# One core, an FFT convolution beside a state-space scan: the hand-planned order of steps is replaced by a finer one, with six pooled buffer slots and a swap issued from two queues

## The chip, the cores and the metric

The kernel runs on one core of a Trainium2 chip. The metric is device time in microseconds (us); a time given for the kernel is the median of several executions. The profile is of one execution and gives the span from its first to its last instruction.

The engines are PE (TensorE, matrix products into PSUM), DVE (VectorE), ACT (ScalarE), POOL (GpSimd) and SP (SyncE). In this kernel POOL and SP do nothing but issue DMA transfers, apart from a few constants that POOL makes at the start.

## The reference, cut to what matters

There are two independent halves on sequences of 2048 steps with 1024 channels; the outputs are laid side by side.

```
# A: a 4-tap shift filter, a gate, and a long causal convolution by FFT
k_shift = sum_t k_pad[:, t:t+S, :] * shift_k[:, ks-1-t]
kv = k_shift * v
y  = irfft(rfft(pad(kv)) * rfft(pad(ssm_k)))[:S] + kv * ssm_D
a  = q * y
# B: a complex diagonal state-space layer, 1024 states
Bu = x @ B_bar.T ;  h = Lam_bar * h + Bu[t] ;  hseq = stack(h)
b  = 2 * Re(hseq @ C.T) + x * Dskip
return concatenate([a, b], axis=-1)
```

## The kernel before, in words

The whole program is a list of small steps written out by hand in the string `ORDER` (lines 65 to 164 of the kernel before). Each word names a step, its indices and the buffer slots that it takes: `U.3.1:p6` is step `U` for chunk 3, part 1, in PSUM slot p6; `lh.5:h0` is a load into slot h0. The loop at L728 reads the words from left to right and calls the step, so the string fixes the order of the instructions on each engine. Between engines there is no common order: an engine runs ahead until the next instruction in its own list has to wait for data or for a slot whose former tenant is still being read. So a load that stands late in the string may be issued long before its neighbours, if SP has nothing to wait for.

Half B goes in 16 chunks of 128 time steps. For chunk i:

- `x.i` (L441) loads the chunk transposed, by a DMA transpose on SP.
- `U.i.jp` (L453), four steps of 32 matmuls, 128x128 each, multiplies by B (`BT`); `ue.i.jp` (L455) is the ACT copy out of PSUM.
- `r1` and `r2` (L465, L474) rotate into real form on DVE, `sc` (L483) is the scan, two instructions, one for the real and one for the imaginary half, with the carry into the next chunk (L487, L488, added in `r2` at L476), and `r3`, `r4` (L465, L495) rotate back.
- `y.i.dh.part` (L506, L511) multiplies by C (`CT`) and adds the skip term; `ye` (L521) copies out on ACT and `yst` (L523) stores, issued by POOL.

Half A goes in stages that each need all of the stage before:

- `kp` and `vp` (L529, L537) load rows of k and v. `kvm` (L546) multiplies by the four filter taps, and `kva` (L553, L555, L556) sums the taps and multiplies by v: three DVE instructions in one step. `am` (L565) is the first short transform on PE, `ae` (L574) the ACT copy, and `ast` (L576) stores to the DRAM scratch `Ys_kv`, issued by POOL.
- `hl`, `hT`, `hc`, `hm`, `he`, `hst` (L580 to L624) do the same for the filter `ssm_k`, into `Ys_h`.
- Second stage, 32 groups g. `lh`, `lk` (L634) load two groups of `Ys_h`, `Ys_kv` in one transfer of 512 KB, and `lw` (L629) the weights of two groups, all issued by SP. `sh`, `sk` (L641) transform; `she`, `ske` (L651, L660) copy out on ACT. `sw.g` (L665, L666) is the swap: the tile `hab` holds a spectrum of 128 partitions (real part in 64, imaginary part in 64), and two transfers from SBUF to SBUF write a copy with the halves exchanged. Both are issued by POOL. `pr.g` (L671) multiplies the two spectra on DVE, and `sa.g` (L680) transforms back; `sae` (L689) copies out and `vst` (L693) stores to the scratch `Vs`.
- Third stage: `vl` (L698) loads from `Vs`, `a3` (L710) finishes the transform, `a3e` (L718) copies out, `qm` (L722) multiplies by q (`qp`, L703), `ost` (L726) stores.

At the start there are `ld_par`, `ld_w`, `wb`, `wbe` (parameters and filter taps), `bl`, `bT`, `bc` (load, transpose and copy of B into `BT`), `cl`, `cT`, `cc`, `cx` (the same for C, `cx` by DMA transpose) and `tabA1`, `sin1`, `eo`, `stt`, `z1`, `z2` (rotation tables).

Slots: p0 to p7 are the PSUM banks, b0 to b14 SBUF tiles of 256 KB, a0 to a10 of 512 KB, m0 and m1 the products of DVE, w0 to w2 the weights. A pool `a1` holds `kring` (rows of k) and the taps `wbc`; when its last reader is done, pool `a2` takes its place with the slots h0 to h2 and k0 to k2, which serve `lh` and `lk` alone (L633).

Of the kernel before, what the change touches and what calls it, by code (L numbers as in the profile page):

```python
# [14 lines left out]
ALU = mybir.AluOpType  # L15
# [7 lines left out]
NG = 32  # L23
# [51 lines left out]
ae.1.0:b8 cx.5.0 cT.3.0:p0 ast.0.1 ae.1.2:b13 U.2.3:p1 kvm.2:m1 cc.3.0 hl.2.0:a4 ae.1.3 cT.0.0:p7 ae.1.1 ast.1.1 cT.3.1:p2 lw.0:w0 ue.2.3 r2.0:a5
hT.0.1:p6 ast.1.0 cc.0.0 cT.2.0:p0 kva.2:b14 hT.0.2:p3 cc.3.1 hT.0.3:p5 cc.2.0 U.3.0:p1a0 hl.1.1:a6 hc.0.1:b11 sc.0 hc.0.3:b10 am.2.0:p7 am.2.1:p2
am.2.2:p0 am.2.3:p6 ae.2.0:b12 cx.6.1 hm.0.3.0:p5 ae.2.1 hm.0.3.1:p7 ae.2.2:b7 hm.0.3.2:p2 ast.2.0 ae.2.3 x.4:b6 cT.0.1:p0 he.0.3.2:b5 U.3.1:p6
ast.2.1 cc.0.1 he.0.3.0:b14 kvm.3:m0 kp.3 he.0.3.1 U.3.2:p2 ue.3.1 hst.0.3.0 ue.3.0 hc.0.2:b13 r3.0:m1 U.3.3:p0 x.6:b4 ue.3.2 ue.1.3 hm.0.2.0:p5
ue.3.3 hm.0.2.1:p7 hd.0 hm.0.1.0:p6 r4.0 hm.0.3.3:p1 he.0.2.0:b8 hm.0.0.0:p3 x.5:b12 hm.0.0.1:p2 he.0.1.0:b10 hm.0.2.2:p4 hm.0.2.3:p0 he.0.0.0:b7
hm.0.1.1:p5 r1.1:m1 y.0.0.0:p6 he.0.0.1 he.0.1.1 y.0.0.1 hst.0.0.0 he.0.3.3 he.0.2.1 x.7:b13 y.0.0.2 he.0.2.2:b14 r2.1:a7 hst.0.3.1 he.0.2.3 y.0.0.3  # L80
hl.2.1:a9 lw.2:w1 hm.0.0.2:p3 sc.1 hm.0.0.3:p2 hst.0.2.1 hT.1.0:p5 ye.0.0:b0 hT.1.1:p1 lw.1:w2 hm.0.1.2:p7 y.0.1.0:p4 hst.0.2.0 y.0.1.1 hst.0.1.0
he.0.0.2:b7 y.0.1.2 x.9:b3 he.0.0.3 y.0.1.3 r1.2:m1 hm.0.1.3:p0 ye.0.1 hT.1.2:p6 hst.0.0.1 hc.1.0:b11 hT.1.3:p3 U.4.0:p2a10 vp.7:a5 hc.1.3:b5 hd.1
r2.2:a3 yst.0 hc.1.2:b14 hm.1.0.0:p4 hm.1.0.1:p5 sc.2 ue.4.0 vp.3:a6 hm.1.0.2:p3 hm.1.0.3:p6 U.4.1:p2 he.0.1.2:b11 he.0.1.3 he.1.0.0:b8 hst.0.1.1
he.1.0.1 U.4.2:p7 ue.4.1 hst.1.0.0 hc.1.1:b10 U.4.3:p0 ue.4.2 r3.1:m1 he.1.0.2:b7 hm.1.1.0:p4 hm.1.1.1:p5 ue.4.3 hm.1.1.2:p2 hm.1.1.3:p1 he.1.0.3
hm.1.3.0:p7 r4.1 hm.1.3.1:p3 hm.1.3.2:p0 he.1.1.2:b10 hT.2.0:p6 hst.1.0.1 he.1.1.3 hm.1.3.3:p2 kva.3:b0 he.1.1.0:b5 y.1.0.0:p1 he.1.1.1 hst.1.1.1
y.1.0.1 y.1.0.2 he.1.3.2:b11 r3.2:m1 hst.1.1.0 vp.6:a8 he.1.3.3 y.1.0.3 y.1.1.0:p4 hst.1.3.1 ye.1.0:b8 r1.3:m0 y.1.1.1 am.3.0:p5 hc.2.0:b2 am.3.1:p0
# [12 lines left out]
hst.3.2.0 ue.6.1 kva.8:b2 hc.3.0:b5 hm.3.1.0:p6 hm.3.1.1:p7 hm.3.1.2:p4 ast.7.1 ue.6.2 hm.3.1.3:p2 hT.3.3:p5 he.3.1.0:b8 U.6.3:p3 he.3.1.1 r4.4
hc.3.3:b11 hst.3.1.0 kvm.9:m0 he.3.1.2:b10 y.4.0.0:p0 he.3.1.3 ue.6.3 am.8.0:p1 hst.3.1.1 am.8.1:p6 ae.8.0:b14 am.8.2:p7 am.8.3:p5 kvm.10:m1 y.4.0.1  # L100
ae.8.1 ae.8.2:b1 ast.8.0 y.4.0.2 ae.8.3 y.4.0.3 ast.8.1 kva.9:b2 kp.7 y.4.1.0:p4 ye.4.0:b8 y.4.1.1 kva.10:b10 am.9.0:p2 x.11:b14 am.9.1:p3 ae.9.0:b6
am.9.2:p1 am.9.3:p6 y.4.1.2 ae.9.1 ae.9.2:b2 y.4.1.3 ast.9.0 ae.9.3 kvm.11:m0 hm.3.3.0:p7 ast.9.1 ye.4.1 am.10.0:p5 am.10.1:p0 am.10.2:p2 ae.10.0:b1
hm.3.3.1:p3 yst.4 hm.3.3.2:p1 ae.10.1 am.10.3:p6 hm.3.3.3:p4 ae.10.2:b10 U.9.0:p5a10 kvm.12:m1 ast.10.0 ae.10.3 he.3.3.2:b11 ast.10.1 he.3.3.3
U.9.1:p0 he.3.3.0:b6 hd.3 hst.3.3.1 ue.9.0 kva.11:b2 he.3.3.1 hm.3.0.0:p2 hst.3.3.0 ue.9.1 hm.3.0.1:p6 hm.3.0.2:p1 hm.3.0.3:p4 he.3.0.0:b8 U.7.0:p7a6
he.3.0.1 kva.12:b1 he.3.0.2:b5 hst.3.0.0 he.3.0.3 am.11.0:p5 ue.7.0 am.11.1:p3 am.11.2:p0 am.11.3:p2 ae.11.0:b10 hst.3.0.1 U.7.1:p6 kvm.13:m0 ae.11.1
ae.11.2:b11 ae.11.3 ast.11.0 U.7.2:p1 ue.7.1 ast.11.1 kvm.14:m1 U.7.3:p4 ue.7.2 kva.13:b2 am.12.0:p7 ue.7.3 am.12.1:p5 am.12.2:p3 am.12.3:p0
ae.12.0:b6 U.8.0:p2a0 ae.12.1 kva.14:b8 ae.12.2:b5 ast.12.0 ae.12.3 am.13.0:p6 ue.8.0 am.13.1:p1 ast.12.1 am.13.2:p4 am.13.3:p7 ae.13.0:b10 U.9.2:p5
r1.5:m0 ae.13.1 ae.13.2:b11 ast.13.0 ae.13.3 am.14.0:p3 ue.9.2 am.14.1:p0 ast.13.1 am.14.2:p2 am.14.3:p6 ae.14.0:b1 kvm.15:m1 U.8.1:p1 ae.14.2:b2
ae.14.1 ae.14.3 ast.14.0 U.8.2:p4 ue.8.1 r2.5:a3 ast.14.1 lh.0:h0 lh.1:h1 lh.2:h2 kva.15:b6 U.8.3:p7 ue.8.2 U.9.3:p5 ue.8.3 sc.5 am.15.0:p3 ue.9.3
am.15.1:p2 am.15.2:p0 sh.0.0:p6 ae.15.0:b8 sh.0.1:p1 sh.1.0:p4 ae.15.1 am.15.3:p7 sh.1.1:p5 ae.15.2:b5 U.11.0:p3a4 lh.4:h0 ast.15.0 ae.15.3 she.0.0:a9  # L110
ast.15.1 she.0.1 r1.6:m0 sh.2.0:p2 she.1.0:a2 sh.2.1:p0 sw.0 sh.4.0:p7 she.1.1 sh.4.1:p6 sh.5.0:p1 she.4.0:a8 sh.5.1:p4 sh.3.0:p5 she.5.0:a7 lh.3:h2
# [55 lines left out]
def full_kernel(ctx, tc, A_q, A_k, A_v, A_shift_k, A_ssm_k, A_ssm_D, B_x, B_Lre, B_Lim, B_Bre, B_Bim,  # L167
                B_Cre, B_Cim, B_log_dt, B_Dskip, out, cfg=None):
    c = dict(CFG)
# [83 lines left out]
    def k4(name, shape):  # L253
        return rtile(ring, "a", name, shape)
# [115 lines left out]
    def z2():  # L370
        nc.scalar.mul(Z2[:, 2, :, :], Z2[:, 0, :, :], -1.0)
        for n_ in ("vc", "vs", "rn", "ang"):
            st.pop(n_)
# [419 lines left out]
```

## Time and profile before

| what | value |
|---|---|
| time, three executions | 390.65, 391.42, 395.95 us; median 391.42 us |
| span of the profiled execution | 394.4 us (its own time is not marked among the three) |
| PE busy, matmuls | 366.3 us, 93% of the span, 3529 matmuls |
| DVE busy | 331.7 us, 84% |
| ACT busy | 280.4 us, 71% |
| POOL busy | 126.9 us, 32% |
| bytes moved by DMA | 101.38 MB, mean 257 GB/s |
| transfers issued by SP: share of the 16 DMA engines' span | 54.5%, 58.73 MB |
| transfers issued by POOL: the same | 33.1%, 42.10 MB |

Matmuls overlap each other, so a busy PE is not the same as a PE that starts a matmul as often as it can. The spacing from one start to the next, in a stretch without waits, says what a matmul costs. The chain of waits gives this spacing, since it merges matmuls that follow each other. "PEld" is the load of a matmul's weights, which overlaps the matmuls. In "windows" rows the columns are: stretch, its length, busy time (and count) of each engine, granted TensorE clock, busy share of the DMA engines, GB/s.

### The profile page before, as it was taken

What the parts mean: (1) busy time and instruction counts of PE and PEld (TensorE: products, weight loads), DVE (VectorE), ACT (ScalarE), POOL (GpSimd) and SP (SyncE); (2) the same over time, 40 slices, a digit from 0 to 9 for tenths busy, and PEclk for the clock granted to TensorE, in tenths of its full rate; (3) what the DMA queues carried; (4) which work ended last, traced back from release to release, by engine and by line L of the source; (5) the groups of instructions that cost most, each with busy time, mean ns of one, the idle gap of its engine ahead of it and who ended that gap; (6) DMA issues with size and microseconds to landing.
All of it is one profiled execution on the core that took longest, in us unless ns stands there. A gap on an engine that the chain in (4) does not pass through costs nothing.

```text
span 394.4 us, 8923 instructions
## 1 busy us (share of the span) xinstructions
PE 366.3 (93%) x3529; PEld 246.4 (62%) x3529; DVE 331.7 (84%) x335; ACT 280.4 (71%) x519; POOL 126.9 (32%) x220
## 2 busy tenths in 40 slices
PE   4998998999988999999899699899998989999994
PEld 2898886775737858897366244455546458685441
DVE  4766999899989999999999979889956971999941
ACT  4899997676649969769289559589693994344642
POOL 3000124574716765425213233233240341020142
PEclk9999999999999999999999989999998999999999
DMA  6999999999986767368999997999989868458895
GB/s 192 313 250 290 328 234 280 297 239 373 303 199 225 220 190 249 125 199 295 270 269 296 276 239 244 236 330 268 321 244 284 253 161 295 161 181 285 292 359 216
DMA packets 59076, 101.38 MB, mean 257 GB/s; under 512 B 31102, under 2 KB 33150, under 8 KB 59036
## 3 DMA queue, kind: packets, MB, share of 16 engines
q1 hardware_dynamic: 45308, 58.73, 54.5%
q0 software_dynamic: 13728, 42.10, 33.1%
q8 instruction: 27, 0.44, 0.5%
q14 instruction: 13, 0.11, 0.1%
HBM read 52.57 MB, written 33.55 MB: 218 GB/s over the span
## 4 chain that ended last, share of the span: by engine, by line
PE 23%; issue 19%; DMA 12%; POOL 5%; ACT 3%; DVE 3%; POOLq 0%; SPq 0%; ACTq 0%; DVEq 0%
PE ps_y L506 7%; PE ps_a L641 5%; PE ps_a L680 5%; PE ps_u L453 5%; DMA l2k<-Ys_kv 4%; DMA l2h<-Ys_h 3%; DMA wts<-a_c_W 2%; POOL out_dram L726 2%; DMA hab<-hab 2%; ACT hab L651 1%; POOL Ys_kv L576 1%; DMA Ys_kv<-ysb 1%; DVE mt L546 1%; ACT x L660 1%; PE ps_a L565 0%
## 5 line engine op out<-in xcount | busy, mean ns | idle before, releaser
L506 PE MATMUL ps_y<-CT,h 128*128 128x512 bf16 x512 | 127.2, 381 | 1.3 <-DVE h L495 1.3
L453 PEld LDWEIGHTS <-BT 128*128 128x128 bf16 x2048 | 118.6, 99 | 6.1 <-issue 1.8
L453 PE MATMUL ps_u<-xT,BT 128*128 128x128 bf16 x2048 | 122.0, 220 | 0.4
L506 PEld LDWEIGHTS <-h 128*128 128x128 bf16 x512 | 46.0, 98 | 49.9 <-DVE h L495 2.2
L483 DVE TENSOR_TENSOR_SCAN h<-rtab,h 128x1024 bf16<-128x1024 f32 x32 | 71.5, 2274 | 0.2
L455 ACT CAST u<-ps_u 128x512 bf16<-128x512 f32 x64 | 39.9, 645 | 23.1 <-PE ps_u L453 21.5
L624 POOL DMA_DIRECT2D Ys_h<-ysbh x64 | 46.1, 723 | 23.4 <-ACT ysbh L617 20.6
L671 DVE TENSOR_TENSOR hab<-x,hab 128x2048 bf16<-128x2048 bf16 x32 | 38.8, 1222 | 17.4 <-DMA hab<-hab 11.0
L576 POOL DMA_DIRECT2D Ys_kv<-ysb x32 | 17.5, 549 | 87.2 <-ACT ysb L574 87.0
L465 DVE TENSOR_TENSOR mt<-u,Z 128x4096 bf16<-128x4096 bf16 x16 | 36.6, 2286 | 10.5 <-ACT u L455 10.2
L689 ACT CAST vsb<-ps_a 128x512 bf16<-128x512 f32 x64 | 36.0, 638 | 7.8 <-PE ps_a L680 7.8
L660 ACT CAST x<-ps_a 128x512 bf16<-128x512 f32 x64 | 36.9, 665 | 5.9 <-PE ps_a L641 5.8
L651 ACT CAST hab<-ps_a 128x512 bf16<-128x512 f32 x64 | 35.9, 679 | 7.1 <-PE ps_a L641 7.1
L617 ACT CAST ysbh<-ps_a 128x512 bf16<-128x512 f32 x64 | 34.6, 633 | 8.9 <-DMA Ys_h<-ysbh 5.2
L574 ACT CAST ysb<-ps_a 128x512 bf16<-128x512 f32 x64 | 34.3, 634 | 8.8 <-DMA Ys_kv<-ysb 6.1
L521 ACT CAST yo<-ps_y 128x512 bf16<-128x512 f32 x32 | 19.2, 611 | 26.9 <-PE ps_y L506 25.2
L465 DVE TENSOR_TENSOR mt<-h,Z 128x4096 bf16<-128x4096 bf16 x16 | 36.5, 2284 | 0.0
L680 PE MATMUL ps_a<-hab,wts 128*128 128x512 bf16 x128 | 32.4, 379 | 3.8 <-DVE hab L671 3.5
L546 DVE TENSOR_TENSOR mt<-kring,wbc 128x4096 bf16<-128x4096 bf16 (+3 forms) x16 | 29.9, 1884 | 3.4 <-DMA kring<-in_A_k_dram 3.4
L665 POOL DMA_DIRECT2D hab<-hab x32 | 16.8, 526 | 47.1 <-ACT hab L651 45.0
L511 PE MATMUL ps_y<-Dd,xT 128*128 128x128 bf16 x128 | 28.0, 219 | 0.0
L641 PEld LDWEIGHTS <-wts 128*128 128x128 bf16 x128 | 12.1, 99 | 21.0 <-DMA wts<-a_c_W 3.9
(110 smaller groups left out, 448.0 us busy)
## 6 DMA issues: line engine op xcount, KB each, us to landing
Ys_kv<-ysb POOLq DMA_DIRECT2D x32, 256.0 KB, 3.8
Ys_h<-ysbh POOLq DMA_DIRECT2D x64, 128.0 KB, 4.3
l2h<-Ys_h SPq DMA_DIRECT2D x16, 512.0 KB, 6.7
hab<-hab POOLq DMA_DIRECT2D x64, 128.0 KB, 6.7
l2k<-Ys_kv SPq DMA_DIRECT2D x16, 512.0 KB, 6.6
Vs<-vsb POOLq DMA_DIRECT2D x16, 512.0 KB, 4.9
vv<-Vs SPq DMA_DIRECT2D x32, 256.0 KB, 4.2
hk<-in_A_ssm_k_dram SPq DMA_DIRECT2D x8, 512.0 KB, 8.7
```

Source lines behind the costliest of these rows:

```text
L453: nc.tensor.matmul(pu[:, w, jl, :], BT[:, 2 * jp + jl, w, d, :], xT[:, d, :], start=(d == 0), stop=(d == ND - 1))
L455: E["ue"] = lambda i, jp: nc.scalar.copy(st["u", i][:, :, 2 * jp:2 * jp + 2, :], st.pop(("pu", i, jp))[:])
L465: nc.vector.tensor_mul(m, s_, win(Z))
L483: nc.vector.tensor_tensor_scan(gf[:, a * W:(a + 1) * W], rt1, gf[:, a * W:(a + 1) * W], 0.0, ALU.mult, ALU.add)
L506: nc.tensor.matmul(py[:], h[:, 1 - w, j, :], CT[:, j, w, dh * 512:(dh + 1) * 512], start=(j == 0 and w == 0), stop=(j == NJ - 1 and w == 1))
L617: nc.scalar.copy(st["yh", qd, n4, w // 2][:, :, w % 2, :], st.pop(("pa", qd, n4, w))[:].rearrange("p (c d) -> p c d", c=2))
L624: gpd(Ys_h[cc, n0:n0 + 2, :, qd * DQ:(qd + 1) * DQ].rearrange("n k d -> k n d"), t_[:, cc, :, :])
L651: nc.scalar.copy(st["hab", g][:, 0, cols], pt[:])
L660: nc.scalar.copy(st["x16", g][:, w * 512:(w + 1) * 512], st.pop(("ps", "l2k", g, w))[:])
L671: nc.vector.tensor_mul(hab[:], st.pop(("x16", g))[:].unsqueeze(1).to_broadcast([P, 2, D]), hab[:])
L680: nc.tensor.matmul(pt[:], st["w", gq][:, gi, 1 + a, :], hab[:, a, w * 512:(w + 1) * 512], start=(a == 0), stop=(a == 1))
L689: nc.scalar.copy(st["vsb", gq][:, gi, w * 512:(w + 1) * 512], st.pop(("ps", "v", g, w))[:])
```

## The change

- The string `ORDER` is written anew: 1722 words for 1565 before. Every transfer, matmul, copy and vector instruction of before is still there, as often as before.
- Steps are cut finer. `U` takes one state block of 16 matmuls for 32 (same PSUM tile, same single copy `ue`). `kva` becomes `kva`, `kvb`, `kvc`. The scan becomes `sc.i.0`, `sc.i.1`, then `cm`, `ca` (the carry), and `rc` is the addition of the carry. Other steps may now stand between these.
- The slots h0 to h2 and k0 to k2 go, and a11 to a16 come in pool `a2`. `lh` and `lk` take any slot a0 to a16, and so may `u`, `hab`, `vsb`, `vv`, `qt` and the others of that size.
- The swap's first half is issued by SP, in the same queue as the loads; the second half stays with POOL.
- `st.pop` becomes `st[...]` and the unused option `actsw` goes; neither makes an instruction.

```
-CFG = {'kr': 8, 'bdve': 4, 'actsw': ()}
+CFG = {'kr': 8, 'bdve': 4}
+NA = 11
...
-ld_par ld_w:a0a1 ld_G bl.2.0:b0 ld_sd bl.0.1:b1 bl.2.1:b2 ld_F x.0:b3 wb.4:p0 bl.3.0:b4 wb.0:p1 bl.7.1:b5 wbe.4 par_T:p2 bl.5.0:b6 wbe.0 bl.5.1:b7
+ld_w:a0a1 wb.0:p0 wb.3:p1 wbe.3 cl.2.0:b0 bl.2.1:b1 wb.2:p2 ld_par par_T:p3 bl.3.0:b2 p32 exp1 dve2 wb.6:p4 exp2 wbe.2 wbe.6 wb.1:p1 dve3 sm_pre sin0
...
+bl.3.1:b6 wb.7:p4 cc.2.0 bl.1.0:b7 bT.1.0:p6 x.1:b8 bT.3.1:p7 bc.1.0 wb.4:p0 U.1.0.0:a5p5 wbe.4 x.3:b9 U.3.0.0:a6p3 bl.2.0:b0 bT.2.0:p6 dd U.3.0.1
+x.0:b10 wb.5:p0 U.0.0.0:a7p2 wbe.7 bc.2.1 bc.2.0 bc.3.1 U.1.1.0:p6 U.1.1.1 U.1.0.1 U.0.1.0:p7 U.3.1.0:p1 U.0.0.1 wbe.5 sin1 tabA2 sin2 par_rest eo
+kp.-1 kp.0 kvm.1:m0 ue.1.0 kp.1 kvm.2:m1 U.0.1.1 kva.1 U.3.1.1 ue.3.1 ue.1.1 bl.4.1:b5 ue.0.0 x.2:b2 U.2.1.0:p0 bT.4.1:p5 bc.4.1 bl.4.0:b6 bT.4.0:p1
...
     def k4(name, shape):
-        return rtile(ring, "a", name, shape)
+        if cur["a"][0] < NA:
+            return rtile(ring, "a", name, shape)
+        return rtile(ap_pool("a2"), "a", name, shape)
...
-    def U(i, jp):
-        if jp == 0:
+    def U(i, jp, jl):
+        if (jp, jl) == (0, 0):
             st["u", i] = k4("u", [P, 2, NJ, T])
-        pu = ptile("ps_u", [P, 2, 2, T])
...
+        if jl == 0:
+            st["pu", i, jp] = ptile("ps_u", [P, 2, 2, T])
+        pu, xT = st["pu", i, jp], st["xT", i]
+        for w in range(2):
+            for d in range(ND):
+                nc.tensor.matmul(pu[:, w, jl, :], BT[:, 2 * jp + jl, w, d, :], xT[:, d, :], start=(d == 0), stop=(d == ND - 1))
...
+    def sc(i, a):
+        gf = st["g", i][:].rearrange("p a j t -> p (a j t)")[:, a * W:(a + 1) * W]
+        nc.vector.tensor_tensor_scan(gf, rt1, gf, 0.0, ALU.mult, ALU.add)
...
+    def kvb(n2):
+        m = st["km", n2]
+        st["kv", n2] = k2("acc")
+        nc.vector.tensor_add(st["kv", n2][:], m[:, 0, :], m[:, 1, :])
...
     def l2(nm, Ys, gq):
-        st[nm, gq] = rtile(ap_pool("a2"), nm[2], nm, [P, GC, D])
+        st[nm, gq] = k4(nm, [P, GC, D])
         spd(st[nm, gq][:], Ys.rearrange("c n (s g) d -> (c n s) g d", g=NG)[:, gq * GC:(gq + 1) * GC, :])
...
     def sw(g):
         hab = st["hab", g]
-        gpd(hab[0:64, 1, :], hab[64:128, 0, :])
+        spd(hab[0:64, 1, :], hab[64:128, 0, :])
         gpd(hab[64:128, 1, :], hab[0:64, 0, :])
```

Two rows of the new string from the middle of the second stage show how loads (`lh.6:a6`, `lh.7:a11`), spectra (`she.12.0:a5`, `she.13.0:a12`) and the state layer's tiles share the slots:

```
+ye.7.0:b10 sw.11 pr.11 rc.8 sa.11.0:p1 sa.11.1:p2 ue.12.0 sc.8.1 lw.6:w0 sk.12.1:p7 sk.12.0:p6 sae.11.1 sk.13.0:p3 ske.12.0:b14 U.12.2.0:p5 lh.6:a6
+sh.13.0:p2 sc.8.0 cm.8 ca.8 sh.12.0:p4 rc.9 sh.12.1:p6 sc.9.1 sc.9.0 r3.8:m1 she.12.0:a5 she.12.1 U.12.2.1 vst.4 ue.12.2 lh.7:a11 she.13.0:a12 lw.7:w2
```

## Prediction, made before the changed kernel was run

> **What bounds the kernel now.** I read the stretches first, then the chain, then the waits of PE, DVE and SP. The stretches (columns: length, then busy time and count of PE, PEld, DVE, ACT, POOL; clock; DMA share; GB/s):
>
> ```profile
> 0.00:20.00 20.00, 14.86 (x116) 10.67 (x117) 12.53 (x53) 13.75 (x20) 3.66 (x12) 1.00 0.94 250
> 20.00:40.00 20.00, 18.80 (x334) 18.46 (x332) 13.17 (x24) 20.00 (x37) 0.00 (x0) 1.00 1.07 275
> ...
> 160.00:180.00 20.00, 19.50 (x293) 16.96 (x291) 19.58 (x19) 13.20 (x26) 4.79 (x9) 1.00 0.56 192
> 220.00:240.00 20.00, 16.89 (x77) 7.48 (x78) 16.53 (x14) 11.46 (x23) 4.26 (x8) 0.91 0.95 251
> 280.00:300.00 20.00, 17.84 (x102) 8.99 (x100) 13.70 (x12) 13.32 (x27) 5.80 (x11) 0.97 0.94 261
> 340.00:360.00 20.00, 20.00 (x196) 13.23 (x194) 19.83 (x18) 7.72 (x15) 2.71 (x5) 1.00 0.63 201
> ```
>
> PE is the bound nearly everywhere, DVE a second one up to 200 us: it idles 14.3 us in the first 40, then hardly at all. At 220 and 280 both have holes and the clock drops; from 340 on PE has none.
>
> What PE's work is worth without holes comes from the spacing of matmuls in the chain:
>
> ```profile
> 201.37 1.79 PE ps_u L453 x32
> 203.16 1.73 PE ps_a L680 x8
> ...
> 216.43 10.49 DMA l2h<-Ys_h
> 226.96 2.29 PE ps_a L641 x5
> ```
>
> That is 0.056 us for 128 columns and 0.216 us for 512. Counts from the groups: 896 matmuls of 512 columns (512 of L506, 128 each of L680 and L641, 64 each of L565 and L710) are 193.5 us; 2048 of L453 are 114.7; 128 of L609 at half of 0.216 are 14.0; 128 of L511 are 7.2; 320 transposes at about 0.06 are 19; eight of L403 at about 0.5 are 4. Sum 353 us. The first matmul starts at 5.1 us, and about 5.4 us follow the last one (copy and store of the last tile). So the 394.4 us are 5.1 + 353 + 5.4 + 31 us of lost PE time. The 31 are all that an order can win.
>
> ```profile
> PE ps_a L680 <- DVE hab L671: 3.5, 3, 1.9
> PE ps_a L565 <- DVE acc L556: 2.8, 4, 1.9
> PE ps_a L641 <- DMA l2h<-Ys_h: 2.3, 1, 2.3
> ...
> DVE mt L546 <- DMA kring<-in_A_k_dram: 3.4, 1, 3.4
> ...
> SPq L634 <- PE ps_a L641: 47.2, 19, 6.1
> ```
>
> Columns: total us, times, longest. PE's waits are many and short, so none of them is "the" bottleneck. SP mostly waits for a slot that PE still reads. By place, starts of matmuls against the spacing above lose about 9 us up to 80, 8 from 80 to 200, and 14 from 200 to 330, of which two drops of the clock are part.
>
> **The change part by part.**
>
> *Finer steps, renamed slots, dropped options.* No engine gets an instruction more or less; a third of `kva` costs on DVE what it cost inside. Nothing by itself: it only allows other orders.
>
> *The new start.* The first multiplication with taps (L546) began at 34.23 us, after waiting for a load of k that SP issued only at 27.73:
>
> ```profile
> 34.23 2.29 DVE L546 TENSOR_TENSOR mt<-kring,wbc 128x4096 bf16<-128x4096 bf16 x1 [3.37 <-DMA kring<-in_A_k_dram]
> ```
>
> ```profile
> 27.73 0.38 SPq L529 DMA_DIRECT2D kring<-in_A_k_dram  x1
> ```
>
> In the new string SP issues that load 19th. Ahead of it stand four parameter rows (0.33 us each), nine loads (0.45), three transposes (1.35, then about 2 each) and two pieces of k (1.05 together): 0.7 + 1.3 + 4.1 + 5.4 + 1.1 = 12.6 us. It landed 6.4 us after its issue before; so at about 19. DVE has 16 us of work ahead of it (memset 1.8, small ones 2.5, tables 5, diagonal and decay table 1.9, four copies at 0.6, parameters 2.2), starting at about 7: 21 to 22. Before, 19 us of DVE work were done by 34.2. So DVE would be 34.2 - 19 - (22 - 16) = 9 us further. PE cannot take all of it. Counting PE and DVE work in the string up to each step of PE that needs DVE (`am`, `y`, `sa`), the smallest surplus of PE work over DVE work between 30 and 170 us of work was 3.1 and is 0.7 now: DVE's lead is partly spent. ACT, full between 20 and 60 before (20.00 and 19.95 of 20), now runs the tables' 16 small scalings with six U tiles waiting to be copied, which may stall PE 1 to 3 us. I take 5 us of gain by 165 us. Bounds: 7.5 (9 less 2.4, with ACT hidden, and a little of the load waits) and -2 (the early transposes collide with the loads of B, PE stalls at its first U as it did not before).
>
> *Loads in the second and third stage.* For each load I count the PE work between the release of its slot (or of the slot of any load ahead of it on SP) and its first reader. Smallest values, before and now: `lh` 5.9 and 10.9 us, `lk` 7.4 and 9.1, `vl` 5.8 and 9.5, `lw` 5.2 and 6.0 (mean 7.0 and 7.6). Landings took 6.7, 6.6, 4.2 and 8.0 us in the median, up to 10.49 and 13.86 in the chain. So `lh` and `vl` go out of danger, `lk` mostly, `lw` hardly: it keeps three slots. The holes that the chain puts on these loads are about 1 us at 197, 1 at 220 and 2.5 at 227, the weights' several of 0.2 to 1.1. I take 5 of them, with the clock drop after 227. Bounds 7 and 1.
>
> The drop: at 220 to 230 the row has PE busy 6.89 of 10 and a clock of 0.85, at 290 to 310 0.94 and 0.89.
>
> ```profile
> 220.00:230.00 10.00, 6.89 (x28) 0.85 1.07 229
> 290.00:300.00 10.00, 8.05 (x51) 0.94 1.02 261
> 300.00:310.00 10.00, 10.00 (x80) 0.89 0.86 303
> ```
>
> Each is some 3.4 us at half speed, 1.7 us lost, behind holes of only 2 to 2.5 us. (The Trainium skill, "TensorE: Matmul & The Clock Gate", Part 1, puts the step down after at least one idle window of about 3.4 us; by that rule no hole here should have cost a drop, and the 1.7 us would not come back. The row decides.)
>
> *The swap.* Each group's chain is copy out (two of about 0.5 us apart, 1.2 in all), issue 0.5, landing, `pr` 1.2:
>
> ```profile
> DMA hab<-hab: 14.0, 12
> ...
> DMA to landing us min/median/max: 2.2/6.7/10.4
> ```
>
> (the hab tile: idle time that the swap ended, us and times; landings). With 6.7 that makes 9.7 us. PE work from the end of `sh` to the start of `sa` is at least 7.3 before and 8.6 now, in the median 13.9 and 13.6; ten groups of 32 lie under 11 before, eight now. Now half the swaps stand in SP's queue. SP pays 32 issues of about 0.37, 12 us, hidden in its 47.2 us of waiting for PE; what is behind a waiting load on SP waits too, and six halves stand behind a load or weight whose slot comes free later than the half itself is ready, by 0.9 to 8.4 us of PE work (`sw.3`, `sw.15` to `sw.19`); the distances of these groups, 13.2 to 18.4, still cover 9.7 and that by 0.2 to 3.5. POOL drops 32 issues of 0.526, 16.8 us: worth nothing, POOL is busy 32%. Before, PE's waits for `pr` and its copy were 3.5 and 1.2, with one clock drop of 1.7. I take 2 us of gain. Bounds: 5 and, if landing on SP's queue is slower, see the second rival.
>
> (The Trainium skill, "DMA: Bandwidth & Descriptors", section "Issuing engines are not separate DMA queues", says that transfers started by several engines run on the same 16 DMA engines and that only issue time is saved. By it the split is worth the 0.5 us of one issue per swap at most and would not shorten a landing; no row here shows a swap issued by SP.)
>
> *The end.* The last `U` and the last `y` are 15.7 us of other PE work apart; DVE and ACT need about 15 for the chunk between. Same tail of 5.4. Nothing.
>
> Sum: 394.4 - 5 - 5 - 2 = 382.4 us of span. The median of the runs is 3.0 below the span (391.4), so **379.4 us**. It leaves PE 19 us of holes.
>
> **The rivals.**
>
> *A, no change.* DVE, not the start, limits to 200 us, and its lead is eaten by ACT; the loads gain while SP's longer list loses. For it: DVE busy 19.6 of 20 at 160 to 180. Against it: the holes after 200 are on PE with DVE at 16.53 and 13.70. Gain 0 to 7.5: 384 to 392.
>
> *B, slower: a half swap lands behind loads in its own queue.* SP now puts a 128 KB half behind `lk` and `lh` of 512 KB; three of those took 13.86 us to land. For it: the chain's row; against it: halves on POOL's queue already share with stores and took 6.7. The median group has 13.6 - 9.7 = 3.9 us to spare, so it decides from landings of about 10.6. Swaps come in seven bursts; at a landing of 13.9 each burst loses 3.3 us, as its first `sa` holds back PE: 23 us, and with 5 won at the start 391 + 18 = 409. At about 12.3 us it eats the gain of 12.
>
> *C, better: PE without holes as from 340 on,* but for the first 9 us and the weights: holes of 10 us, 373 span, 370 us.
>
> **How the numbers follow.** Forecast, 375 to 384: 0.47. A: 0.25. B: 0.16, most of it between 392 and 415. C, 366 to 375: 0.12. Two in ten left out, half on each side, gives 370 to 397. 2% (about what a measurement can tell) is 383.6 and 399.2: faster 0.45 + 0.12 = 0.57; same 0.02 + 0.25 + 0.04 = 0.31; slower 0.12. Where only cases that gain hold, 370 to 384.
>
> **What would show it.** Right: the first L546 starts near 22 us; DVE idles under 9 us in the first 40; no PE wait for l2h above 1 us; clock 1.00 from 220 to 310; hab lands in 7 us on both queues. Wrong: PE's holes grow in 20 to 60 (ACT), or "DVE hab <- DMA hab" goes far above 11.0 us with hab landings over 10 (B), or SP waits in front of a swap. I am wrong as well if the new order delays a chunk of the state layer so that DVE's idle time only moves.

## The result, and the profile after

| | before | after |
|---|---|---|
| time, median (executions) | 391.42 us (390.65 to 395.95, 3) | 375.63 us (374.92 to 376.57, 3) |
| ratio | | 0.9582, 95% interval 0.9482 to 0.9683 |
| profiled execution: time, span | about 396 (see below), 394.4 us | 374.92, 372.7 us |
| PE, DVE, ACT, POOL busy | 93, 84, 71, 32% | 95, 88, 75, 30% |
| granted TensorE clock | drops at 220 to 230 and 290 to 310 | 1.00 up to 360 us |
| landing of a swap half, median, longest | 6.7, 10.4 us | 4.0, 7.3 us |

Line numbers of the kernel after are higher by up to 11 in the first steps and lower by up to 12 in the last: L453 is L462, L546 is L553, L641 is L642, L665 and L666 are L661 and L662, L671 is L667, L680 is L676, L710 is L702.

Stretches after, with the columns of the prediction's first fence:

```profile
0.00:20.00 20.00, 14.85 (x183) 12.12 (x184) 15.06 (x56) 14.35 (x22) 3.16 (x11) 1.00 0.93 259
20.00:40.00 20.00, 20.00 (x362) 20.00 (x360) 19.89 (x30) 19.37 (x36) 0.00 (x0) 1.00 1.11 291
160.00:180.00 20.00, 19.20 (x241) 14.92 (x243) 18.44 (x16) 16.18 (x32) 5.93 (x12) 1.00 0.93 259
220.00:240.00 20.00, 19.84 (x213) 14.05 (x214) 19.78 (x17) 17.22 (x34) 4.83 (x9) 1.00 0.80 254
280.00:300.00 20.00, 19.84 (x172) 12.32 (x174) 15.38 (x11) 17.37 (x35) 5.08 (x10) 1.00 0.89 261
340.00:360.00 20.00, 18.12 (x106) 9.10 (x106) 14.73 (x12) 10.99 (x22) 3.94 (x8) 1.00 0.72 265
220.00:230.00 10.00, 9.95 (x105) 6.85 (x104) 9.80 (x10) 8.10 (x17) 1.65 (x3) 1.00 0.81 279
290.00:300.00 10.00, 9.89 (x122) 7.64 (x123) 9.93 (x8) 8.59 (x18) 4.04 (x9) 1.00 0.88 274
300.00:310.00 10.00, 9.95 (x62) 5.08 (x61) 8.33 (x8) 7.40 (x16) 1.52 (x4) 1.00 0.96 302
```

Three things are to be seen. DVE is full from 20 us on (busy 15.06 + 19.89 us of the first 40, where it had 25.7). PE has no holes at 220 and 280, where it had 16.89 and 17.84 of 20. And the clock column is 1.00 in every row. The timeline shows why DVE is full early: k's first loads are issued at 12 to 14 us, and the multiplication finds its data there, without a wait ahead of it.

```profile
12.15 0.58 SPq L538 DMA_DIRECT2D kring<-in_A_k_dram  x1
...
20.21 4.49 DVE L553 TENSOR_TENSOR mt<-kring,wbc 128x4096 bf16<-128x4096 bf16 x2
```

All of PE's waits after, and two of SP's (total us, times, longest):

```profile
PE ps_a L413 <- DMA hk<-in_A_shift_k_dram: 4.5, 1, 4.5
PE ps_a L702 <- ACT ot L708: 1.8, 1, 1.8
PE ps_a L573 <- ACT ysb L580: 1.4, 2, 0.9
PE ps_a L612 <- ACT ysbh L618: 1.1, 1, 1.1
PE ps_a L612 <- ACT yo L528: 1.0, 1, 1.0
PE ps_a L573 <- DVE mt L560: 0.8, 1, 0.8
PE ps_t L427 <- ACT wbc L417: 0.6, 1, 0.6
PE ps_a L573 <- ACT ysbh L618: 0.4, 1, 0.4
PE ps_a L612 <- ACT hT L600: 0.3, 1, 0.3
...
SPq L661 <- ACT x L656: 21.9, 9, 4.4
SPq L661 <- ACT hab L650: 21.4, 9, 4.1
```

PE's waits for `hab`, `acc` and `l2h`, 3.5, 2.8 and 2.3 us before, are not in the list any more, nor any for a load of the second stage. The first row is the start, which before had too (5.1 us). What SP mostly waits for now is the copy ahead of a swap half; before it was slots that PE still read. The prediction named "SP waits in front of a swap" as a sign of being wrong. It came, 43.3 us of it in these two rows, but PE waits neither for a swap nor for a load of the second stage.

To place the gain I use one more measure. For each step of PE, the PE work ahead of it (by the spacings of the prediction: 0.056 us for 128 columns, 0.216 for 512) is subtracted from the time at which it starts in the trace. The result is the PE time lost up to there. It begins with the 5 us before the first matmul and contains the clock drops; span = 353 + lost + a tail of 5 to 6 us (9 in one kernel below).

```
us lost at PE work of    20    40    80   120   160   200   240   280   300   end   span
before                  9.5  11.0  13.4  18.5  19.7  23.9  29.4  33.9  36.2  36.0  394.4
after                   5.8   5.6   6.1   9.8  12.8  12.7  12.5  12.6  12.6  14.3  372.7
```

So 6.9 us come from the part up to 160 us of work, and 16.7 from the stretch 160 to 300, in which the kernel after loses nothing; 1.9 are given back near the end. One caution: an execution's span is 1.7 to 2.3 us below its time wherever both are known here, so the span of 394.4 belongs to an execution of about 396 us, some 5 above the median. Further executions of before, 7, 17 and 19 in three groups, had medians of 390.83, 390.59 and 391.39. Of the 21.7 us between the two spans, some 5 are therefore that execution's own; the gain in the medians is 15.8. Nor is the gain the two drops of the clock: two of the further executions of before had a mean granted clock of 1.000 and took 390.71 and 391.39 us.

### The profile page after: what moved, and what is told of

Its sections match the earlier page's. It is cut to its first block, busy times and chain, and to the rows that moved or that the text cites. A ratio compares the mean times of both kernels' runs of the same rounds, so it can differ in the third digit from the quotient of the medians.

```text
span 372.7 us, 8839 instructions
## 1 busy us (share of the span) xinstructions
PE 352.9 (95%) x3486; PEld 243.2 (65%) x3529; DVE 328.2 (88%) x335; ACT 280.5 (75%) x519; POOL 110.5 (30%) x188
## 2 busy tenths in 40 slices
DMA packets 60100, 101.38 MB, mean 272 GB/s; under 512 B 31102, under 2 KB 33150, under 8 KB 60060
## 4 chain that ended last, share of the span: by engine, by line
PE 69%; DMA 11%; ACT 6%; issue 6%; POOL 5%; DVE 1%; POOLq 0%; SPq 0%; ACTq 0%
PE ps_u L462 26%; PE ps_y L517 19%; PE ps_a L676 7%; PE ps_a L642 7%; DMA Ys_h<-ysbh 6%; POOL Ys_h L625 4%; DMA Ys_kv<-ysb 3%; PE ps_t L427 3%; PE ps_a L702 2%; PE ps_y L522 2%; ACT ot L708 2%; ACT ysb L580 1%; PE ps_a L573 1%; ACT ysbh L618 1%; PE ps_a L612 1%
## 5 line engine op out<-in xcount | busy, mean ns | idle before, releaser
L462 PEld LDWEIGHTS <-BT 128*128 128x128 bf16 x2048 | 120.2, 98 | 13.0 <-issue 1.5
L462 PE MATMUL ps_u<-xT,BT 128*128 128x128 bf16 x2048 | 126.9, 219 | 0.5
L517 PE MATMUL ps_y<-CT,h 128*128 128x512 bf16 x490 | 124.8, 379 | 0.7
L464 ACT CAST u<-ps_u 128x512 bf16<-128x512 f32 x64 | 38.3, 616 | 18.0 <-PE ps_u L462 17.4
L667 DVE TENSOR_TENSOR hab<-x,hab 128x2048 bf16<-128x2048 bf16 x32 | 38.4, 1221 | 11.7 <-ACT x L656 9.5
L580 ACT CAST ysb<-ps_a 128x512 bf16<-128x512 f32 x64 | 36.0, 633 | 6.6 <-PE ps_a L573 3.3
L582 POOL DMA_DIRECT2D Ys_kv<-ysb x32 | 17.5, 550 | 74.5 <-ACT ysb L580 74.4
L474 DVE TENSOR_TENSOR mt<-h,Z 128x4096 bf16<-128x4096 bf16 x16 | 36.5, 2284 | 0.1
L676 PE MATMUL ps_a<-hab,wts 128*128 128x512 bf16 x125 | 32.5, 379 | 0.2
L662 POOL DMA_DIRECT2D hab<-hab x32 | 16.9, 529 | 52.4 <-ACT hab L650 35.6
L553 DVE TENSOR_TENSOR mt<-kring,wbc 128x4096 bf16<-128x4096 bf16 (+3 forms) x16 | 30.0, 1883 | 0.1
L612 PE MATMUL ps_a<-hT,F1t 128*128 128x256 bf16 x128 | 20.2, 272 | 2.4 <-ACT ysbh L618 1.1
```

The costliest lines, as they stand in the source:

```text
L462: nc.tensor.matmul(pu[:, w, jl, :], BT[:, 2 * jp + jl, w, d, :], xT[:, d, :], start=(d == 0), stop=(d == ND - 1))
L464: E["ue"] = lambda i, jp: nc.scalar.copy(st["u", i][:, :, 2 * jp:2 * jp + 2, :], st["pu", i, jp][:])
L474: nc.vector.tensor_mul(m, s_, win(Z))
L517: nc.tensor.matmul(py[:], h[:, 1 - w, j, :], CT[:, j, w, dh * 512:(dh + 1) * 512], start=(j == 0 and w == 0), stop=(j == NJ - 1 and w == 1))
L580: nc.scalar.copy(st["ysb", n2, cc][:, dh * 512:(dh + 1) * 512], st["pa", n2, w][:])
L667: nc.vector.tensor_mul(hab[:], st["x16", g][:].unsqueeze(1).to_broadcast([P, 2, D]), hab[:])
```

## The experiments

Twelve kernels, each timed beside the kernel before. "Lost" is the measure above.

### The start alone: the rows of k loaded late again

```
-kp.-1 kp.0 kvm.1:m0
+bl.4.1:b5 x.2:b2 bl.4.0:b6 bl.5.1:b7 bl.7.0:b0 bl.5.0:b1 bl.6.0:b4 x.4:b3 bl.6.1:b11 cl.3.1:b12 bl.7.1:b13 x.5:b14
+kp.-1 kp.0 kvm.1:m0
```

> New order, but twelve loads and transposes that followed the first rows of k on SP are put ahead of them, so that these rows are issued near 25 us in place of 12 and land near 31 as in the kernel before. Theory (DVE's early start is what won the head): DVE is 8 to 10 us later, PE loses 5 to 7 more by 160 us of work and keeps them: 380 to 383 us. Rival (the head's gain is PE's own, from the first transposes and U): 375 to 377.

Measured: 387.08 us (385.22 to 388.31), ratio to before 0.9921 (0.9893 to 0.9949); span 384.9, 12.2 above the kernel after. The first L553 in its timeline:

```profile
30.41 4.49 DVE L553 TENSOR_TENSOR mt<-kring,wbc 128x4096 bf16<-128x4096 bf16 x2 [10.36 <-DMA kring<-in_A_k_dram]
```

PE's longest waits in that kernel:

```profile
PE ps_a L573 <- DVE acc L568: 6.0, 1, 6.0
PE ps_a L413 <- DMA hk<-in_A_shift_k_dram: 4.4, 1, 4.4
PE ps_t L427 <- ACT CT L447: 2.3, 1, 2.3
```

DVE lost 10.36 us there, and PE lost 10.3 more than after by 40 us of work (15.9 against 5.6), 12.1 by 160, 12.2 at the end. Of the 10.3, 6.0 are PE's wait for DVE in the list; behind it the granted clock is at half for 6.8 us (46.87 to 53.70 us), worth up to 3.4. So a late DVE at the start reaches PE about whole, clock included, which is more than the 5 to 7 us that I expected, and it is not made up: DVE is busy 17.9 to 19.9 of each 20 us from 40 to 160 and has little slack to catch up with. What the twelve loads that now come first do by themselves was not separated.

### The finer steps: joined again in the new order

```
-kvm.2:m1 U.0.1.1 kva.1 U.3.1.1 ue.3.1 ue.1.1
...
-stt kvb.1:b6
+stt kva.1 kvb.1:b6
...
-r3.0:m1 sc.1.0 U.5.0.0:a5p3 sc.1.1
+r3.0:m1 U.5.0.0:a5p3 sc.1.0 sc.1.1
...
     def U(i, jp, jl):
...
+            return
         pu, xT = st["pu", i, jp], st["xT", i]
-        for w in range(2):
-            for d in range(ND):
-                nc.tensor.matmul(pu[:, w, jl, :], BT[:, 2 * jp + jl, w, d, :], xT[:, d, :], start=(d == 0), stop=(d == ND - 1))
+        for jl in range(2):
+            for w in range(2):
+                for d in range(ND):
+                    nc.tensor.matmul(pu[:, w, jl, :], BT[:, 2 * jp + jl, w, d, :], xT[:, d, :], start=(d == 0), stop=(d == ND - 1))
```

> New order, but the finer steps joined again: the two halves of U run together where the second stood, kva with kvb, the two scans together. Theory (fine steps only fill holes): 376 to 379 us. Rival (finer steps are what keeps PE fed): 381 to 386, with lost PE time growing between 20 and 160 us of work.

Measured: 389.50 us (387.48 to 390.14, ten executions), ratio 0.9972 (0.9941 to 1.0004); span 387.0. The loss is 10.3 at 40 us of work (after: 5.6), 19.6 at 120 (9.8) and 24.4 at 160 (12.8), then nearly as flat as after. In the joined version ACT waits longer for `U` tiles; ACT's waits in this kernel:

```profile
ACT u L466 <- PE ps_u L464: 31.5, 29, 5.6
```

and in the kernel after:

```profile
ACT u L464 <- PE ps_u L462: 17.4, 17, 5.6
```

Joining costs 14 us in this order, more than even the rival expected. But the order was planned for fine steps, and a joined step stands where its later part stood, so this is not what fine steps win over an order planned for coarse ones. Three kinds of step were joined at once, so which of them counts stays open too.

### The swap's queues, in both orders

Both halves on POOL in the new order; both on SP in the new order; the split in the old order (with its old slots):

```
-        spd(hab[0:64, 1, :], hab[64:128, 0, :])
+        gpd(hab[0:64, 1, :], hab[64:128, 0, :])
```

```
-        gpd(hab[64:128, 1, :], hab[0:64, 0, :])
+        spd(hab[64:128, 1, :], hab[0:64, 0, :])
```

```
-        gpd(hab[0:64, 1, :], hab[64:128, 0, :])
+        spd(hab[0:64, 1, :], hab[64:128, 0, :])
```

> New order and slots, both swap halves issued by POOL as before. Theory (the split is worth the 0.5 us of one issue per swap, mostly hidden): 375 to 378 us, hab landing back near 6 us without effect on PE. Rival (the split made the second stage's gain): 383 to 388, with PE waiting for pr again.

> New order and slots, both swap halves issued by SP. Theory: 375 to 379 us, SP has the time. Rival (halves behind 512 KB loads land late): hab landing above 7 us in the median and 380 to 390.

> Old order and old slots, only the first half of each swap issued by SP. Theory: within 2 us of 391.4; some halves wait behind loads that wait for a slot, so rather 392 to 396. Rival (the split itself shortens the landing from 6.7 to 4 us and so made the second stage's gain): 380 to 385.

| kernel | time | ratio to before | span | landing of hab, median, longest |
|---|---|---|---|---|
| after (split) | 375.63 | 0.9582 (0.9482 to 0.9683) | 372.7 | 4.0, 7.3 |
| new order, POOL | 380.83 | 0.9805 (0.9722 to 0.9887) | 378.9 | 4.3, 8.6 |
| new order, SP | 380.47 | 0.9738 (0.9672 to 0.9804) | 375.6 | 4.0, 7.7 |
| old order, split | 393.92 | 1.0104 (1.0030 to 1.0178) | 391.0 | 6.4, 10.8 |

The landing falls with the order, whichever engine issues: 6.4 to 6.7 in the old one, 4.0 to 4.3 in the new one. The split shortens it by 0.3 at most. Yet in the new order POOL alone costs 5 us, between the 378 of my theory and the 383 of the rival. The loss is that of the kernel after up to 160 us of work (13.4 against 12.8) and grows from 14.1 to 19.1 between 260 and 300. POOL's timeline there, with both halves on POOL:

```profile
300.66 0.54 POOL L685 DMA_DIRECT2D Vs<-vsb  x1 [3.68 <-ACT vsb L683]
301.20 0.53 POOL L661 DMA_DIRECT2D hab<-hab  x1
...
303.78 0.52 POOL L662 DMA_DIRECT2D hab<-hab  x1
304.30 0.56 POOL L530 DMA_DIRECT2D out_dram<-yo  x1
305.11 0.53 POOL L661 DMA_DIRECT2D hab<-hab  x1 [0.25 <-ACT hab L650]
308.34 0.52 POOL L662 DMA_DIRECT2D hab<-hab  x1 [2.71 <-issue]
```

and in the kernel after, where POOL issues only the second halves:

```profile
297.66 0.55 POOL L685 DMA_DIRECT2D Vs<-vsb  x1 [4.17 <-ACT vsb L683]
298.20 1.57 POOL L662 DMA_DIRECT2D hab<-hab  x3
...
302.11 0.53 POOL L662 DMA_DIRECT2D hab<-hab  x1 [1.78 <-ACT hab L650]
```

Six halves (301.20 to 303.78) stand behind a store that waits 3.68 us for ACT, and then leave one by one; with the split three stand behind that store, and the other three have left from SP. That looks like the cause, but it is not what PE waits for: the six have landed by 307.34, and PE uses their groups without a wait. PE's waits for the swap in that kernel are two, of 1.1 and 3.3 us, at two other groups:

```profile
PE ps_a L676 <- DVE hab L667: 4.5, 2, 3.3
```

```profile
289.18 1.22 DVE L667 TENSOR_TENSOR hab<-x,hab 128x2048 bf16<-128x2048 bf16 x1 [3.22 <-DMA hab<-hab]
...
315.25 1.23 DVE L667 TENSOR_TENSOR hab<-x,hab 128x2048 bf16<-128x2048 bf16 x1 [4.00 <-DMA qt<-in_A_q_dram]
```

```profile
316.54 1.47 PE L676 MATMUL ps_a<-hab,wts 128*128 128x512 bf16 x6 [3.32 <-DVE hab L667]
```

For the first, the halves are issued at 280.19 and 280.72, as soon as ACT's copy is there, and land 8.6 and 8.3 us later, with loads under way that SP issued from 278.88 on; in the kernel after, the same halves leave at 278.34 and 278.60, before those loads, and the second lands in 4.9. For the second, the late half is the one issued at 308.34, after a pause of POOL of 2.71 us that no event in the trace explains; it lands at 315.08. (The row names a load of q, which this multiplication doesn't read.) These waits are 4.5 of the 6.1 us of lost time between the two kernels. So the split takes PE's waits for the swap away, but that the place behind a store did it is not shown, and one execution doesn't tell whether the pause returns.

With both halves on SP the loss is no larger than after (13.4 in all). The profiled execution took 377.75 us; its span is longer only behind the last matmul, where about 9 us follow in place of about 5. The median of that kernel, 380.47, is not explained by its trace, and its interval touches that of the kernel after. In the old order the split costs 1.04% of the time, as expected. PE's waits for the swap fall there too, from 3.5 to 1.2 us, but it now waits for weights, 6.9 us where it was 1.3:

```profile
PE ps_a L642 <- DMA wts<-a_c_W: 6.9, 4, 3.5
```

For the longest, the load is issued at 212.43, just behind two swap halves (211.26 and 211.90), and lands 8.3 us later. That the halves delay it is my reading; no run isolates it.

### The slots alone

The old order and the old swap, but slots chosen anew in 399 of the 899 words that take one, each time the slot released longest ago by the order of the string. That moves 120 of the 158 tiles of 512 KB, which now share 17 slots, but also 152 of the 200 of 256 KB and 124 of the 497 in PSUM:

```
-kvb.2:b14 kvc.2 hT.0.2:p3 cc.3.1 hT.0.3:p5 cc.2.0 U.3.0.0:p1a0 U.3.0.1 hl.1.1:a6 hc.0.1:b11
+kvb.2:b6 kvc.2 hT.0.2:p3 cc.3.1 hT.0.3:p5 cc.2.0 U.3.0.0:a0p1 U.3.0.1 hl.1.1:a6 hc.0.1:b14
```

> Old order throughout, both swap halves on POOL, but the 17 big slots pooled, each step taking the one that was released first. Theory (order, not slots): 388 to 392 us. Rival (pooled slots let the loads start early, in any order): l2h and l2k waits of PE go, 379 to 384.

Measured: 415.08 us (407.68 to 420.46; the spread leaves no ratio with an interval), span 413.4. Neither theory nor rival expected that. The loss is 55 us, and PE waits for swaps above all:

```profile
PE ps_a L676 <- DVE hab L667: 12.0, 7, 3.4
```

No step has another place in the order; only who waits for whose slot has changed, and that costs some 17 us (lowest time) to 24 (median). The slots are part of the plan as much as the order.

### One half of the order new, the other old

First with all slots chosen anew in that way, then with every slot of the first half as in its own kernel and the second half's kept wherever free. The cut is the last store of the products of k and v (about 165 us of work). The string at the cut, old behind new, then new behind old:

```
-am.14.0:p1 ae.14.0:b9 ast.15.1 ae.14.3 ast.14.1 am.14.1:p5 U.8.3.0:p4
+am.14.0:p1 ae.14.0:b9 ast.15.1 x.10:b11 x.12:b13 U.7.2.1 U.7.3.0:p4
```

```
-ae.15.3 she.0.0:a9 ast.15.1 she.0.1 r1.6:m0 sh.2.0:p2 she.1.0:a2
+ae.15.3 she.0.0:a9 ast.15.1 she.1.0:a14 she.1.1 ue.11.0 sh.2.1:p7
```

With all slots anew:

> New order up to the last store of the first stage (word ast.15.1), then the steps that are left in the old order, both swap halves on POOL, slots dealt out again. By the lost PE time the head won 6.9 us by 160 us of work. Theory (start 7, second stage 9 to 15, from the order): 384 to 386 us, lost PE time near 13 at 160 and growing to about 30 at 300. Rival (all of it comes from the second stage once PE and DVE have lead): the tail loses less too, 378 to 381.

> Old order up to the same word, then the new order, swap split between SP and POOL, slots pooled. Theory: lost PE time near 20 at 160, then flat: 380 to 384 us. Rival (the second stage runs clean only because of the lead won at the start): lost time grows on after 160, 387 to 391.

Measured: 427.20 us (ratio 1.0928, 1.0862 to 1.0993) and 404.48 (1.0263, 1.0152 to 1.0375). Between 40 and 120 us of work they lose 25.0 and 19.5 us, where the two kernels that they are made of lose 4.2 and 7.5, so the slots spoil them as in the kernel above. None of the expected ranges is met, and they tell little of the halves. With the slots kept:

> New order up to the last store of the k/v products (about 165 us of TensorE work) with its own slots throughout, old order and old swap (both halves on GpSimd) after that; a slot of the tail is its own wherever that is free (402 of 484), else the one released longest ago. Theory: the gain has two independent halves. Lost TensorE time is that of the changed kernel up to 160 us of work (5.8 at 20, 7 to 8 at 100, 12 to 14 at 160), then grows as in the old order, by 14 to 17 up to 300: 27 to 31 in all, a span of 385 to 390, 387 to 392 us. Rival 1, the second half only lost because DVE entered it without a lead: with the new head the loss stays under 17, 375 to 380 us. Rival 2, the slots that had to be changed decide: it loses more than the old order did after 160 (over 20 us), 395 us and up.

> Old order up to the last store of the k/v products with its own slots throughout, new order and the split swap after that, tail slots its own wherever free (415-odd of 500). Theory of two independent halves: lost time is the old one up to 160 us of work (9.5 at 20, 13 at 60 to 100, 19 to 21 at 160), and from 180 on flat within 3 us: 21 to 25 in all, a span of 379 to 383, 381 to 386 us. Rival 1, the head carries all: it grows after 160 as before, 389 to 393 us. Rival 2, slots decide: over 393 us.

Measured: new head, old tail 394.45 us (390.79 to 398.03, ten executions; ratio 1.0056, 1.0011 to 1.0100), old head, new tail 411.90 us (1.0473, 1.0397 to 1.0550). In the first kernel 402 slots of 484 in the tail were kept, in the second 393 of 475, so 82 had to change in each.

```
us lost at PE work of    20    40    80   120   160   200   240   280   300   end   span
before                  9.5  11.0  13.4  18.5  19.7  23.9  29.4  33.9  36.2  36.0  394.4
old order, split swap   8.8   9.8  12.3  16.0  17.5  25.6  30.5  33.2  33.6  33.4  391.0
new head, old tail      6.1   6.0   6.4  10.6  12.4  20.0  25.1  28.6  30.6  30.4  388.9
old head, new tail      9.5   9.9  11.9  15.8  17.3  30.8  38.9  41.6  41.6  50.1  409.5
after                   5.8   5.6   6.1   9.8  12.8  12.7  12.5  12.6  12.6  14.3  372.7
```

The new head with its slots is as good as in the kernel after up to 160 (12.4 against 12.8), and the old tail then loses 18.2 us. The profiled execution (388.9 us of span) took 390.79, 3.7 below its median; the median, 394.45, is 3 us above that of before. So the head's gain doesn't reach the time. The executions of before that were timed beside it go down to 388.41 us; at the same tail of 5.4 us and with the 17.5 to 19.7 lost by 160 as in the table, such a one loses 8 to 11 us behind 160 (an estimate). The old tail thus loses more behind the new head than it need behind its own. Old head and new tail comes out where the rival "slots decide" has it, over 393: the tail loses 24 us up to 300, and 8.5 more behind it, on loads and swaps:

```profile
PE ps_a L642 <- DMA l2k<-Ys_kv: 6.4, 4, 3.0
...
PE ps_a L676 <- DVE hab L667: 3.4, 1, 3.4
PE ps_a L702 <- DMA vv<-Vs: 3.2, 3, 2.7
```

So my theory of two halves that add up is right for the head's lost time, and falls for both tails: the new one was free of holes only behind its own head. Whether that is the 82 slots that had to change or the state of SP, DVE and ACT at the cut was not separated.

### The loads of the middle stage, late again

Twenty-four words `lh` and `lk` moved later, so that less PE work lies between their release and their first reader. Two of them:

```
-U.11.2.1 ue.11.2 lh.2:a8 lh.3:a0 rc.5 sc.5.0
+U.11.2.1 ue.11.2 lh.2:a8 rc.5 sc.5.0
...
-ue.10.0 lw.3:w0 sa.5.0:p0
+ue.10.0 lw.3:w0 lk.3:a3 lh.3:a0 sa.5.0:p0
```

> The changed kernel with 24 loads of the middle stage (lh, lk) moved later in the order, so that the TensorE work between the release they wait for on SyncE and their first reader shrinks from 10.9 to 53 (lh) and 9.1 to 36 (lk) to mostly 5.4 to 8; all else as it is. Landings of these loads took 5.3 and 4.8 us in the median, up to 7.5. Theory that early loads are what keeps TensorE without holes after 200: it loses 4 to 9 us more between 160 and 300, with waits of TensorE for l2h or l2k, 379 to 384 us. Rival, the loads were early enough either way and the position of swaps and copies counts: within 1.5 us, 374 to 377 us, no such waits over 1 us in total.

Measured: 390.92 us (388.39 to 400.2, ten executions), 15.3 above the kernel after; ratio to before 0.9970 (0.9919 to 1.0022). The profiled execution took 400.2 us (span 398.1) with a granted clock of 0.95 from its start, so the sizes in the trace are an upper end. PE's waits:

```profile
PE ps_a L642 <- DMA l2h<-Ys_h: 8.0, 6, 2.3
PE ps_a L642 <- DMA l2k<-Ys_kv: 5.9, 5, 2.2
```

Stretches of 5 us of the same kernel, columns as before:

```profile
200.00:205.00 5.00, 4.40 (x22) 2.07 (x23) 4.27 (x6) 4.14 (x10) 1.27 (x3) 0.95 1.42 308
205.00:210.00 5.00, 2.82 (x16) 1.26 (x15) 4.99 (x3) 3.24 (x8) 0.36 (x1) 0.95 0.76 148
...
215.00:220.00 5.00, 1.10 (x3) 0.32 (x4) 0.00 (x0) 1.28 (x3) 1.98 (x4) 0.73 1.04 253
220.00:225.00 5.00, 5.00 (x29) 3.07 (x28) 3.50 (x3) 2.39 (x5) 0.14 (x1) 0.55 0.52 164
```

Up to 180 us of work the loss is that of the kernel after (13.0 against 12.6); at 300 it is 36.5. The rival, that the loads were early enough either way, falls. The size is well above the 4 to 9 us that I expected. In the profiled execution 24 us are lost between 160 and 300. Of these 13.9 are waits for loads; 10.2 us at half clock (217.59 to 224.41 and 251.72 to 255.13) are worth at most 5.1; and matmuls of 512 columns start 0.224 us apart for 0.216, some 3.7 us for about 460 of them (both estimates). But the clock is not needed: two other executions, with a mean granted clock of 0.998, which has no room for a fall of 3.4 us, took 388.79 and 388.88, still 13 above the kernel after.

The run shows what late loads cost, not what the change won by earlier ones, since it makes them later than they ever were: from issue to first reader the median is 7.2 us for `lh` and 8.0 for `lk`; before it was 19.4 and 15.4, after it is 23.4 and 10.5.

### A wait near the end taken out

Near 349 us PE waits 1.8 us for ACT, which waits for a store that has just been issued from the tile's slot. Six output tiles take slots that have long been free:

```
-a3e.1.0:b14
+a3e.1.0:b9
...
-ye.14.0:b3
+ye.14.0:b13
...
-a3e.11.0:b9 a3e.8.0:b13
+a3e.11.0:b3 a3e.8.0:b14
...
-a3e.2.0:b14
+a3e.2.0:b9
...
-a3e.5.0:b13
+a3e.5.0:b14
```

> The changed kernel with six output tiles of the last stage in other slots, none of which waits for a store that has just been issued (a3e.1, ye.14 and four that follow from these); order unchanged. In the changed kernel ScalarE waited 2.2 and 3.6 us there for such stores to land, and TensorE 1.8 us for ScalarE. Theory: these waits go and the span falls by 1.5 to 2 us, 373 to 374 us. Rival, TensorE is held by the next loads (vv) at the same place: no change, 374.5 to 376.5 us.

Measured: 375.18 us (372.20 to 376.03, four executions), ratio to before 0.9518 (0.9450 to 0.9585). The wait is gone from PE's list, and the loss falls by 0.4 from 160 us of work to the end, where after it rose by 1.5. But this execution had lost 3 us more by 160 (15.8 against 12.8), on the same words in the same order. The difference of the medians, 0.45 us, is well inside the spread, so whether the version is better can't be said.

## Why the prediction was right or wrong

The forecast was 379.4 us, faster; it is 375.63, faster by 4.2%. The direction and the places were right, and so was the size of what the new order gives without the split; the swap was too small and its reason wrong.

- **"Nothing by itself: it only allows other orders" (finer steps): open.** As a statement on the instructions it holds, but no term of the sum stood for what the new order gains by them. Joined again they cost 14 us in this order; against an order planned for coarse steps their worth was not measured.
- **The new start, "I take 5 us of gain by 165 us": about right in size, with the right mechanism.** The first L553 was forecast for 21 to 22 us and started at 20.21. DVE idled 5.1 us of the first 40 (forecast: under 9). The gain is 6.9 us at 160 against before's profiled execution, 4.7 against the old order with the split. I was right that PE can't take all 9 us of DVE's lead. ACT, full from 20 to 60, did not cost what the lower bound feared. The other way round it is dearer: with k late in the new order 12.2 us are lost.
- **Loads of the second and third stage, "I take 5 of them, with the clock drop", bounds 7 and 1: about right in size.** The profile of before has 2.3 us of PE's waits for `l2h` (in the prediction's list) and these:

```profile
PE ps_a L641 <- DMA wts<-a_c_W: 1.3, 2, 1.1
PE ps_a L641 <- ACT hab L651: 1.2, 1, 1.2
...
PE ps_a L641 <- DMA l2k<-Ys_kv: 1.0, 2, 0.7
```

  The loads' are 4.6, and the clock drop that follows the longest is 1.7, so 6.3 in all; after, none of it is left. In the medians the new order with both halves on POOL, which has the start and the loads but not the split, is 10.6 us below 391.42 (9.8 below the kernel before timed beside it): start and loads were 5 + 5. How these 10 divide was not separated.
- **The swap, "I take 2 us of gain", bound 5: the mis-sized term, and wrong in its reason.** In the profile of before PE's waits for the swap and its copy are 3.5 and 1.2 and the clock drop behind one of them 1.7, 6.4 in all; after, none is left. I gave it 2 for fewer late landings on two queues. The landing is the same with one queue (4.3) and with two (4.0), and yet the split is worth 5.2 us by the medians in this order: with POOL alone PE waits 4.5 us for the swap, with the split not at all. The rule I weighed, that transfers from several engines share the same 16 DMA engines and only issue time is saved (the Trainium skill, "DMA: Bandwidth & Descriptors", section "Issuing engines are not separate DMA queues"), agrees with the landings of 4.0, 4.3 and 4.0. But what I worked out from it, 0.5 us per swap at most, is not the worth: one late group left after SP's loads in place of before them, another after an unexplained pause of POOL of 2.71 us. In the old order the same split costs 3 to 4 us.
- **The end, "Nothing": nearly.** One wait of 1.8 us came in near 349.
- **The sum.** 382.4 us of span were forecast and 372.7 measured; the holes of PE are 9.2 us, not 19. That is the span of rival C, "PE without holes as from 340 on" (373), which I gave 0.12. But my 382.4 started from an execution some 5 us above the median, and the 372.7 is not from such a one. The 3.0 that I took off as "the median of the runs below the span" are those 5 less the 2 by which a time exceeds its span; with a profile near the median it would have been 2 added. Between medians I forecast 12.0 us of gain and 15.8 came: 3.8 too little, of which the split is 3.2 (5.2 for 2). That 375.63 lies 0.6 us inside the 375 to 384 of the forecast is luck; one of the three executions, 374.92, lies outside.
- **Rival B**, halves landing late behind SP's loads, needed landings of about 10.6; the longest was 7.3. In the old order something like it may be there, the other way round: weights issued behind swaps, 6.9 us of waiting, and 1% more time.
- **That parts add up** is what the experiments deny most clearly. The head alone wins nothing in the median (394.45), the tail alone costs 20 us (both with 82 slots changed), the split alone costs 3 to 4, other slots alone 17 to 24, and all together win 15.8.

Open: which joined step counts; why the split is worth 5 us in the new order; whether slots or the state at the cut spoil a tail behind the other head; why the kernel with both halves on SP has a median 2.7 us above its profiled execution.

## What to carry to other kernels

Where an order, its buffer slots and its queues were planned together, price a change as a whole by how much PE work stands between each transfer's release and its first reader, and expect late loads to be dear: here 24 of them moved later cost 13 us even where the clock never fell. An engine that is full over a long stretch has little room to win back what it loses at its start (here PE lost 12.2 us behind DVE's 10.4). Before a span is turned into a time, ask which execution the profile shows. And before a queue is blamed for a wait, follow the transfer that the waiting engine really reads.

## What was not expected of the hardware

- The clock falls after shorter holes than I had assumed possible. With the loads late, PE was busy 1.12 us between 214.17 and 217.59 (a hole of 2.30), and the clock stood at half from 217.59 to 224.41; a hole of 2.18 us ten microseconds earlier left it alone. The traces of all fourteen kernels agree on more: the changes of the clock lie on a grid of 3.41 us, each of the 24 falls before the end of PE's work follows a grid step in which PE was busy at most 1.61 us, and no step with less than 1.34 went without one. The hole of 2.18 us lay across two steps, busy 2.21 and 2.43. (The Trainium skill, "TensorE: Matmul & The Clock Gate", Part 1, names one idle window of about 3.4 us; the length agrees, but only one of the 24 steps was idle throughout.)
- In one execution, of the kernel with late loads, the granted clock was 0.95 wherever it was not at half. Matmuls of 512 columns then started 0.224 us apart for 0.216; those of 128 columns stayed at 0.056.
- Transfers of the same size land faster in another order: 128 KB between two SBUF places in 4.0 us in the median in the new order and 6.7 in the old one, with the same 101.38 MB in a shorter time (272 GB/s in the mean against 257). In all kernels here it is 5.9 to 6.7 where the second stage is in the old order and 3.7 to 4.9 where it is in the new one. That the transfers are more evenly spread is my reading; no run isolates it.
- How far the executions of one kernel spread doesn't follow from its holes: 8.3 us for before (388.4 to 396.7, 19 executions) and 1.7 for the kernel after (3), but also 1.6 for the new head with all slots anew (425.77 to 427.39, 4), the kernel with the most lost time.
